# Retention, sparse MoE and slot MoE on one core: x and phi-w2 writes issued later, loads four tiles ahead, end of the branch and slot sums reordered

## The chip, the cores and the metric

The program runs on one core of a Trainium2 chip. The metric is the device time of one execution in microseconds (us); before the change it is 551.8 us, the median of three runs (549.96 to 552.42). Names used below: TensorE (PE) multiplies matrices, VectorE (DVE) and ScalarE (ACT) work elementwise, GpSimd (POOL) works elementwise and issues gathers and scatters, SyncE (SP) issues most of the transfers (DMA). Each engine runs its own instructions in order and waits on semaphores of others.

## The reference

Three layers follow each other. The input is q, k, v of 4 batches, 8 heads, 768 positions and 64 features, and weights in float32.

```python
# 1. retention, head by head, over the sequence
for t in range(S):
    state = gamma * state + k[t] (x) v[t]
    y[t]  = scale * q[t] @ state
x = y, as 3072 tokens x 512 features
# 2. MoE, one expert of 8 per token
e_idx = argmax(x @ w_gate);  gate_w = softmax(x @ w_gate)[e_idx]
eom   = sigmoid(x @ w_output_gate)[e_idx]
out   = gate_w * eom * (relu(x @ w1[e_idx]) @ w2[e_idx])
# 3. slot MoE on that: 8 experts x 4 slots
logits = x @ phi
slots  = softmax(logits, over tokens).T @ x
slots  = relu(slots @ w1[e]) @ w2[e]
out    = softmax(logits, over slots) @ slots
```

## The kernel before

**Stages.** The program has one stage for retention and routing (called the branch here, pool stack `pa`), a conditional part for experts with more tokens than planned (`pv`, not taken with this input), one for the eight experts (`pb`), and one for the slot experts and the output (`pc`). The instructions of an engine stand in the order in which the Python code is written (`manual_schedule`); tile pools set which buffer a tile gets, and an instruction that fills a buffer waits for the last reader of what was in it.

**The branch** goes over 24 tiles of 128 tokens (`NTILE`; 6 chunks of a sequence for each of 4 batches). For a tile i, `load(i)` brings its q, k, v (1 MB, pool `io`); `scores(i)` multiplies k and q, `masks(i)` applies the decay, `out_state` and `out_scores` make the output, and `state` updates the running state. Three tiles are a group (`GROUPS`, `ENDS`): `x_evac` and `x_turn` copy and turn the output, `gate_mm`, `gate_copy`, `gate_sum` make the router's logits, `gate_pick` the choice of expert, `gate_scale` the token's factor, `rank_mm` and `rank` the token's place within its expert. `x_write` multiplies the rows by the factor and stores them to the DRAM tensor `xs` on SP's queue. The list `ORDER` says in which order these steps are written within step i; a name there carries an offset (`"s"` is `scores(i + 1)`, `"xw"` is `x_write(i - 2)`).

Beside this, the branch multiplies phi with the second weights w2 of the eight sparse experts (phi-w2), so that the slot logits can be made from the hidden layer directly. `wq_load(u)` loads a quarter (512 KB) of an expert's transposed w2, 32 quarters in all, `wq_mm(u)` multiplies it, and `wq_put(u)` turns a finished expert and stores it to `wps`. Quarter u is loaded behind step u - 1 and multiplied in step u + 3 (`WLAG`); the quarters that are left behind the last tile follow after the routing.

**End of the branch.** From the ranks a list of rows for each expert is made with the product `lp`, the experts are ordered by their token count (`c8`, `sq8`, `ordf`, `ordi`), and `gather(0)` fetches the rows of the first expert from `xs`, by indirect DMA on POOL. `er` holds the number of the k-th expert in a register of SP, which chooses the weights to load. `limi` holds what the conditional part reads.

**The experts.** Step g = 8 e + f handles block f (128 hidden features) of expert e: `load_w` loads w1 three steps ahead, `split_w` splits it into two parts (ACT and DVE), `l1` makes twelve products and a relu. `behind(e - 1, f)` does the rest of the expert before, a part in each of the eight steps: slot logits, their softmax, `slot_h` (partial sums over tokens, tiles `gps`), `slot_s` (copies `gr` and the sums `gsum`), `slot_t`, and `slot_in` in two halves, which multiplies by w2 (tiles `w`, product `slo`). `load_w2(e, hf)` loads half of w2 (four tiles of 256 KB) into the pool `w2p`, which has four buffers, so a half can be loaded when the half before has been used. `load_m2` brings the weights of the slot experts, up to `NPRE` = 52 of 128 tiles during this stage.

The lines that matter most for SP are the store of x and the loop:

```python
def x_write(i):                       # L547, on SP in step i + 2
    ...
    for a in range(4):
        nc.sync.dma_start(out=xs[...], in_=x[32 * a:32 * a + 32, 0:n]...)   # L557
for i in range(NTILE + 2):            # L579
    load(i + 3)
    for n in ORDER:
        step[n](i)
    ...
    wq_load(i + 1)
```

Of the kernel before, what the change touches and what calls it, by code (L numbers as in the profile page):

```python
# [35 lines left out]
NPRE, NX = 52, 4  # L36
# [99 lines left out]
def retention_moe_kernel(ctx, tc, qt, kt, kn, vn, gates, moe_w1, moe_w2,  # L136
# [47 lines left out]
    whl = ctx.enter_context(tc.tile_pool(name="whl", bufs=3))  # L184
    xp = ctx.enter_context(tc.tile_pool(name="xp", bufs=4))
    xtp = ctx.enter_context(tc.tile_pool(name="xtp", bufs=NX))
# [4 lines left out]
    er = []  # L191
    G = E * KF
# [25 lines left out]


# [27 lines left out]
    with ExitStack() as pa:  # L247
        io = pa.enter_context(tc.tile_pool(name="io", bufs=4))
# [50 lines left out]
        wst = pa.enter_context(tc.tile_pool(name="wst", bufs=6))  # L299
        wtt, wacc = {}, {}  # L300

        def wq_load(u):
            if u < NQ:
                e, q = divmod(u, 4)
                wtt[u] = wst.tile([128, FF], F32, tag="wt", name="wt")
                nc.sync.dma_start(out=wtt[u], in_=moe_w2[1, e, :, q * FF:(q + 1) * FF])

        def wq_mm(u):

            if not 0 <= u < NQ:  # L310
                return
            e, kk = divmod(u, 4)
            if kk == 0:
                wacc[e] = pT.tile([128, 256], F32, tag="w", name="wps")
            t = wtt.pop(u)
            for g in range(4):
                nc.tensor.matmul(out=wacc[e][32 * g:32 * g + 32, :], lhsT=phi[:, kk, :], rhs=t[:, g * 256:g * 256 + 256],  # L317
                                 start=(kk == 0), stop=(kk == KD - 1), skip_group_check=True)

        def wq_put(u):  # L320
            if u % 4 == 3 and 0 <= u < NQ:
                ws = sc2.tile([128, KF, NS], F32, tag="ws", name="ws")
                nc.vector.transpose(out=ws, in_=wacc.pop(u // 4).rearrange("p (f t) -> p f t", t=32))
                nc.sync.dma_start(out=wps[u // 4], in_=ws.rearrange("p f s -> p (f s)"))
# [152 lines left out]
        def gate_pick(i):  # L477
# [5 lines left out]
            lg, og = g[:, :, 0:E], g[:, :, E:2 * E]  # L483
# [3 lines left out]
            nc.vector.tensor_tensor(out=big(1), in0=lg, in1=bc(one_(0), n), op=ALU.subtract)  # L487
            nc.vector.scalar_tensor_tensor(out=big(2), in0=big(1), scalar=0.0, in1=each(con("desc"), n), op0=ALU.is_ge, op1=ALU.mult)
            nc.vector.tensor_reduce(out=one_(3), in_=big(2), axis=AX.X, op=ALU.max)
            nc.vector.tensor_tensor(out=oh[:, t:t + n, :], in0=big(2), in1=bc(one_(3), n), op=ALU.is_equal)  # L490
            for u in range(n):
                nc.vector.tensor_tensor(out=run[:, t + u + 1, :], in0=run[:, t + u, :], in1=oh[:, t + u, :], op=ALU.add)
            nc.vector.tensor_tensor(out=big(4), in0=og, in1=oh[:, t:t + n, :], op=ALU.mult)
            nc.vector.tensor_reduce(out=one_(5), in_=big(4), axis=AX.X, op=ALU.add)
            nc.scalar.activation(out=big(6), in_=big(1), func=ACTF.Exp)
# [15 lines left out]
        def rank_mm(i):  # L511
# [4 lines left out]
            for u in range(n):  # L516
# [3 lines left out]
            nc.tensor.matmul(out=g[:, SC:SC + 4 * n], lhsT=con("same"), rhs=scl.pop(t)[:, 0:n, :],  # L520
                             start=True, stop=True, skip_group_check=True)

        def rank(i):
# [3 lines left out]
            late = t + n == NTILE  # L527
            g = gps.pop(t)
            sm = sc2.tile([128, 3, 4, E], F32, tag="sm2", name="sm2")
            scl[t] = sc2.tile([128, 3, 4], F32, tag="sc", name="sc")  # L530
            nc.vector.tensor_copy(out=scl[t][:, 0:n, :], in_=g[:, SC:SC + 4 * n].rearrange("p (u b) -> p u b", b=4))
# [9 lines left out]
            eng = nc.vector if late else nc.gpsimd  # L541
# [5 lines left out]
        def x_write(i):  # L547
            if i not in ENDS:
                return
            t, n = ENDS[i]  # L550
            s = scl.pop(t)
            x = xr3.pop(t)
            for u in range(n):
                (nc.vector if t + n == NTILE else nc.gpsimd).tensor_tensor(
# [215 lines left out]
    with ExitStack() as pb:  # L770
# [173 lines left out]
        def behind(e, f):  # L944

            if not 0 <= e < E:
                return
# [266 lines left out]
```

## Time and profile before

| What | Value |
|---|---|
| Median of three runs | 551.8 us (549.96 to 552.42) |
| Profiled execution | 553.71 us, its span 551.9 us |
| PE busy | 440.2 us, 80% of the span |
| DVE, ACT, POOL busy | 264.2, 148.3, 129.7 us |
| Moved by DMA | 132.59 MB, mean 240 GB/s |
| SP's queue | 120.24 MB, 63.5% of 16 engines |

The span is the time between the first and the last instruction of the profiled execution; 1.8 us of its time lie outside it. The busy share of an engine is a mean over stages with different limits, so each stage has to be read by itself. "PEclk" in the rows below is the clock that TensorE was granted, as a share of 2.4 GHz (0.50 is 1.2 GHz). "DMA" is the share of time in which the core's 16 DMA engines were busy.

### The profile page before, as it was taken

To read this page: it belongs to the slowest core of one execution; us is meant where nothing else is said; L and a number is where in the kernel's file an instruction comes from. 1 tells how busy PE (TensorE), PEld (TensorE's weight loads), DVE (VectorE), ACT (ScalarE), POOL (GpSimd) and SP (SyncE) were. 2 spreads that over 40 slices of the span, in tenths; PEclk is the share of its full clock that TensorE was granted. 3 is DMA by queue.
4 is the path that set the end of the run, shared out by engine and by line. 5 is a ranking of instruction groups with operands and counts; after the bars stand their busy time and mean duration, and the time that the engine had idled before them with its cause. 6 is when DMAs were issued, how large, how long until landed. Compare 5 with 4: busy or idle time off the path is not lost.

```text
span 551.9 us, 11581 instructions
## 1 busy us (share of the span) xinstructions
PE 440.2 (80%) x4403; PEld 304.2 (55%) x4403; DVE 264.2 (48%) x711; ACT 148.3 (27%) x341; POOL 129.7 (23%) x143
## 2 busy tenths in 40 slices
PE   4793965956856335999999999999999996697993
PEld 3672743645644103888676675867667673234253
DVE  1573744645547501356555546654655654323033
ACT  1431111102102001444344333433334431112033
POOL 2222403504503310203240605124050303020020
PEclk9897878879778555799999999999999999689897
DMA  8957696696674781568293965929395726999958
GB/s 265 399 232 249 214 338 187 240 348 179 261 221 125 209 277 46 160 220 278 90 359 116 313 221 176 331 83 367 106 333 194 268 70 194 364 375 383 361 179 280
DMA packets 71826, 132.59 MB, mean 240 GB/s; under 512 B 8434, under 2 KB 28912, under 8 KB 69456
## 3 DMA queue, kind: packets, MB, share of 16 engines
q1 hardware_dynamic: 65136, 120.24, 63.5%
q0 software_dynamic: 3408, 8.39, 4.4%
q10 hardware_dynamic: 3216, 3.11, 1.7%
q8 instruction: 37, 0.61, 0.5%
q14 instruction: 29, 0.24, 0.1%
HBM read 117.68 MB, written 14.05 MB: 239 GB/s over the span
## 4 chain that ended last, share of the span: by engine, by line
PE 48%; DMA 8%; ACT 2%; DVE 2%; issue 1%; ACTq 0%; SPq 0%
PE hps L809 25%; DMA w<-in_moe_w_dram 5%; PE slo L939 4%; PE gps L918 4%; PE so L1105 3%; PE lps L840 2%; PE fh L1066 2%; PE xps L781 2%; PE ops L1163 1%; DMA ct<-ctok 1%; PE gsum L928 1%; DMA m<-in_moe_w_dram 1%; PE lsum L856 1%; ACT gr L925 1%; PE warm L799 1%; ACT h L814 1%
## 5 line engine op out<-in xcount | busy, mean ns | idle before, releaser
L809 PE MATMUL hps<-xh,wh 128*128 128x416 f32 (+2 forms) x256 | 96.0, 375 | 0.0
L809 PE MATMUL hps<-xh,wl 128*128 128x416 f32 (+2 forms) x256 | 89.6, 350 | 0.0
L809 PE MATMUL hps<-xl,wh 128*128 128x416 f32 (+2 forms) x256 | 89.6, 350 | 0.0
L369 PE MATMUL s<-raw 64*128 64x128 f32 x384 | 36.1, 339 | 41.3 <-DMA raw<-in_qt_dram 11.0
L901 POOL DMA_INDIRECT ctok<-cn,xidx x29 | 28.8, 992 | 170.3 <-DVE cn L898 163.9
L379 DVE TENSOR_TENSOR sS<-s,csa 128x512 f32<-128x512 f32 x48 | 30.9, 686 | 75.1 <-PE s L369 75.1
L216 DVE TENSOR_TENSOR wl<-r,wh 128x512 fp32r<-128x512 f32 x64 | 43.5, 680 | 40.1 <-ACT wh L215 39.7
L809 PEld LDWEIGHTS hps<-xh,wh 128*128 128x128 f32 x256 | 48.7, 190 | 20.9 <-issue 19.6
L814 ACT ACTIVATE h<-hps 128x416 f32<-128x416 f32 (+2 forms) x64 | 32.7, 511 | 99.6 <-PE hps L809 94.7
L369 PEld LDWEIGHTS s<-raw 64*128 64x128 f32 x384 | 30.5, 235 | 43.7 <-issue 36.2
L215 ACT ACTIVATE wh<-r 128x512 fp32r<-128x512 f32 x64 | 39.9, 625 | 52.2 <-ACTq L750 35.3
L809 PEld LDWEIGHTS hps<-xl,wh 128*128 128x128 f32 x256 | 48.9, 191 | 1.7 <-issue 0.8
L809 PEld LDWEIGHTS hps<-xh,wl 128*128 128x128 f32 x256 | 48.6, 190 | 0.8
L632 POOL DMA_INDIRECT xg<-xs,xidx x29 | 30.0, 1035 | 63.6 <-PE xps L781 47.0
L434 ACT COPY xT<-o 128x512 f32<-128x512 f32 x24 | 13.9, 580 | 94.3 <-PE o L402 94.3
L317 PE MATMUL wps<-wt,phi 128*32 128x256 f32 x256 | 26.8, 503 | 15.5 <-DMA wt<-in_moe_w_dram 11.3
L939 PE MATMUL slo<-w,gt 128*32 128x512 f32 x128 | 32.5, 640 | 4.3 <-DMA w<-in_moe_w_dram 3.5
L821 DVE STREAM_TRANSPOSE hB<-h 128x416 f32<-128x416 f32 (+2 forms) x64 | 34.4, 577 | 0.0
L351 POOL TENSOR_TENSOR k<-raw,cs 128x512 f32<-128x512 f32 x20 | 21.0, 1063 | 48.7 <-DMA raw<-in_qt_dram 20.3
L402 PE MATMUL o<-sS,raw 128*64 128x128 f32 x384 | 29.5, 302 | 0.0
L791 DVE TENSOR_TENSOR xl<-xps,xh 128x416 fp32r<-128x416 f32 (+2 forms) x32 | 18.2, 582 | 18.8 <-ACT xh L790 18.2
L1105 PE MATMUL so<-m,hT 128*32 128x320 f32 (+1 forms) x256 | 26.8, 408 | 0.0
(159 smaller groups left out, 575.7 us busy)
## 6 DMA issues: line engine op xcount, KB each, us to landing
m<-in_moe_w_dram SPq DMA_DIRECT2D x128, 256.0 KB, 5.3
wt<-in_moe_w_dram SPq DMA_DIRECT2D x32, 512.0 KB, 7.4
r<-in_moe_w_dram SPq DMA_DIRECT2D x64, 256.0 KB, 4.3
w<-in_moe_w_dram SPq DMA_DIRECT2D x64, 256.0 KB, 4.8
xs<-xr SPq DMA_DIRECT2D x28, 192.0 KB, 3.4
raw<-in_kt_dram SPq DMA_DIRECT2D x5, 1024.0 KB, 8.5
raw<-in_kn_dram SPq DMA_DIRECT2D x5, 1024.0 KB, 9.7
raw<-in_vn_dram SPq DMA_DIRECT2D x5, 1024.0 KB, 9.5
```

The lines of the kernel that those rows point to most:

```text
L215: nc.scalar.activation(out=hi, in_=t, func=ACTF.Copy)
L216: nc.vector.tensor_tensor(out=lo, in0=t, in1=hi, op=ALU.subtract)
L369: nc.tensor.matmul(out=ps[h][:, p, :], lhsT=kq(i, p, 0)[r], rhs=kq(i, p, 1)[r], start=True, stop=True, tile_position=(64 * h, 0), skip_gro ...
L379: nc.vector.tensor_tensor(out=sS[i][:, h], in0=sps.pop((i, h)), in1=con("dm", 128)[:, 4 * h:4 * h + 4, :], op=ALU.mult)
L402: nc.tensor.matmul(out=o_at(i, p, h), lhsT=vals(i, 2 * p + h), rhs=s[:, h, p, :], start=(i % NCH == 0 and n < 4), stop=True, skip_group_ch ...
L632: nc.gpsimd.indirect_dma_start(out=xg[e][j][0:r, :], out_offset=None, in_=xs[:, :], in_offset=bass.IndirectOffsetOnAxis(ap=xidx[0:r, e, j: ...
L809: nc.tensor.matmul(out=ps, lhsT=a[:, kk * 128:(kk + 1) * 128], rhs=x[e][kk][:, 0:c], start=(n == 0), stop=(n == 11))
L814: nc.scalar.activation(out=hs[g][:, 0:c], in_=ps, func=ACTF.Relu)
L821: nc.vector.transpose(out=hB[e][:, 0:NB[e], f, :], in_=hs[e * KF + f][:, 0:c].rearrange("p (b t) -> p b t", t=32))
L901: put = nc.gpsimd.indirect_dma_start(out=ctok[:, :], out_offset=bass.IndirectOffsetOnAxis(ap=xidx[0:r, e, j:j + 1], axis=0), in_=cn[0:r, j ...
L939: nc.tensor.matmul(out=slo[e][32 * i:32 * i + 32, :], lhsT=gts[e][:, hf * 4 + i, :], rhs=w2n[e, hf][i], start=(hf == 0), stop=(hf == 1), s ...
L1105: nc.tensor.matmul(out=so[dh][32 * g:32 * g + 32, :], lhsT=hT[:, f % 4, 32 * hg:32 * hg + 32], rhs=m2_t[64 + e * 8 + f][:, DH[dh]], start= ...
```

## The change

- A fifth buffer for tiles (`io`), and loads four tiles ahead (`load(i + 4)` in step i).
- `x_write` only multiplies (always on POOL); the store is a step of its own, `x_put`, issued at the start of step i + 4. The store of a finished expert's phi-w2 (`wq_put`) is issued at the start of the step behind it.
- `wq_load(i)` at the start of step i, used two steps later (`WLAG` = 2). Only 24 quarters are multiplied in the branch; the eight of the last two experts are loaded in its last steps into 16 buffers of 256 KB (`m2a`, later used for `load_m2`) and multiplied behind the conditional part.
- `rank_mm` and the product that spreads the scale (`scale_mm`) are two steps, behind the phi-w2 product. `gate_pick` is cut in two (`gate_own`), the copy of the scale (`scale_copy`) leaves `rank`.
- At the end of the branch the scale and the store of the last rows go ahead of `rank`, the last store is issued on two queues, and three w1 tiles are loaded ahead of the gather. The numbers of the experts are read one at a time (`load_er`).
- In the experts the slot sums `gsum` go one step behind their copies (`slot_t` in f = 6), the first half of `slot_in` to f = 7 and the second half to f = 1 of the next expert; `load_w2` follows. Four warm-up products instead of eight.

```diff
-WLAG = 3
+WLAG = 2
+NQ0 = NTILE
-ORDER = "xe sc rm s m g1 gc xr w g2 G0 q oq os st G1 rk xw k".split()
-NW0 = 8
+ORDER = "xe sc s m g1 gc xr w rr rs g2 G0 Gb q oq os st G1 rc rk xw k".split()
+ORDER_1 = "xe g1 rr rs rc rk xw gc xr w g2 G0".split()
+NW0 = 4
...
-        io = pa.enter_context(tc.tile_pool(name="io", bufs=4))
+        io = pa.enter_context(tc.tile_pool(name="io", bufs=5))
...
+        def wq_early(u):
+            if NQ0 <= u < NQ:
+                e, q = divmod(u, 4)
+                wtt[u] = []
+                for h in range(2):
+                    t = m2a.tile([128, 512], F32, tag="m2", name="wte")
+                    nc.sync.dma_start(out=t, in_=moe_w2[1, e, :, q * FF + h * 512:q * FF + h * 512 + 512])
+                    wtt[u] += [t[:, 0:256], t[:, 256:512]]
...
+        def x_put(i, queues=(nc.sync,)):
+            if i not in ENDS:
+                return
+            t, n = ENDS[i]
             x = xr3.pop(t)
             for a in range(4):
-                nc.sync.dma_start(
+                queues[a % len(queues)].dma_start(
...
-        for i in range(NTILE + 2):
-            load(i + 3)
-            for n in ORDER:
+        for i in range(NTILE + 1):
+            wq_put()
+            x_put(i - 4)
+            wq_load(i)
+            load(i + 4)
+            if i > NTILE - 4:
+                wq_early(NQ0 + 2 * (i + 3 - NTILE))
+                wq_early(NQ0 + 2 * (i + 3 - NTILE) + 1)
+            for n in ORDER if i < NTILE else ORDER_1:
                 step[n](i)
             decay_table(i + 2)
             if i == 0:
                 late_tables()
-                wq_load(0)
-            wq_load(i + 1)
...
+        scale_copy(i)
+        x_write(i)
+        x_put(i, (nc.sync, nc.scalar))
+        rank(i)
...
+        load_er(0)
+        for g in range(3):
+            load_w(g)
         gather(0)
...
-        for u in range(NTILE + 3, NQ):
-            wq_load(u)
-        for u in range(nq, NQ):
-            wq_mm(u)
-            wq_put(u)
+        wq_turn(NQ0 - 1)
+        wq_put()
...
         def behind(e, f):
+            if f == 1 and 0 < e <= E:
+                slot_in(e - 1, 1)
...
             elif f == 1:
                 logit_sum(e)
-                load_w2(e, 0)
             elif f == 2:
                 p_exp(e)
+                load_w2(e, 0)
...
             elif f == 5:
                 slot_s(e)
-                slot_t(e)
                 c_exp(e)
             elif f == 6:
+                slot_t(e)
+                c_put(e)
+            elif f == 7:
                 slot_in(e, 0)
-                c_put(e)
                 load_w2(e, 1)
-            elif f == 7:
-                slot_in(e, 1)
 
         split_w(0)
+        for u in range(NQ0, NQ):
+            wq_mm(u, ps_1, "lr"[u // 4 % 2])
+            if u % 4 == 3:
+                ws = sp.tile([128, KF, NS], F32, tag="wp", name="ws", bufs=2)
+                nc.vector.transpose(out=ws, in_=wacc.pop(u // 4).rearrange("p (f t) -> p f t", t=32))
+                nc.sync.dma_start(out=wps[u // 4], in_=ws.rearrange("p f s -> p (f s)"))
+        load_er(1)
         keep_warm(w1_t[0][0], NW0, ps_h, "h")
...
         e = E - 1
         logits(e, 1)
         mask(e)
+        slot_in(e - 1, 1)
         load_w2(e, 0)
```

**SP in the middle of the branch.** `xs<-xr` is the store of tiles 6 to 8, `raw` are loads of tiles (the first is tile 13), `wt` a quarter of w2. Before:

```order
L337 DMA raw_831<-in_kn_dram 128x2048
L324 DMA wps_74<-ws_862 128x256
L557 DMA xs_71<-xr_619 32x12x128 x4
L306 DMA wt_913<-in_moe_w2_dram 128x1024
L337 DMA raw_915<-in_kn_dram 128x2048
L306 DMA wt_957<-in_moe_w2_dram 128x1024
L337 DMA raw_959<-in_kn_dram 128x2048
```

Now, from the load of tile 14 on:

```order
L355 DMA raw_837<-in_kn_dram 128x2048
L322 DMA wt_913<-in_moe_w2_dram 128x1024
L355 DMA raw_915<-in_kn_dram 128x2048
L598 DMA xs_71<-xr_623 32x12x128 x4
L322 DMA wt_960<-in_moe_w2_dram 128x1024
L355 DMA raw_962<-in_kn_dram 128x2048
```

The store stood ahead of the load of tile 14; now it stands behind that of tile 15.

**PE behind the conditional part.** `wps<-wte` are products of the last two experts' phi-w2 (their last four of 16 rows are shown), `warm` the warm-up, `xps` the transposes of the gathered rows `xg`. Before:

```order
L670 COMPARE_AND_BRANCH
L670 UNCONDITIONAL_BRANCH
L750 UNCONDITIONAL_BRANCH
L799 MATMUL warm_3740<-wh1_3736 128x512 x8
L781 MATMUL xps_3749<-cs0_65,xg_1934 128x128
```

Now:

```order
L234 MATMUL wps_3749<-wte_1822,phi_75 32x256 x2
L234 MATMUL wps_3749<-wte_1824,phi_75 32x256 x2
L234 MATMUL wps_3749<-wte_1826,phi_75 32x256 x2
L234 MATMUL wps_3749<-wte_1828,phi_75 32x256 x2
L855 MATMUL warm_3779<-wh1_3725 128x512 x4
L837 MATMUL xps_3784<-cs0_65,xg_1977 128x128
```

The products of the last two experts' phi-w2 stand between the conditional part and the warm-up, which has four products instead of eight.

**SP in the experts**, around the end of the second half of expert 0's w2 (tiles `w2`); `r1` is a tile of w1, `m2` one of the slot experts' weights, `wp` the stored phi-w2. Before:

```order
L831 DMA w2_4355<-in_moe_w2_dram 128x512
L206 ISA
L206 DMA r1_4366<-in_moe_w1_dram 128x512
L236 DMA m2_4368<-in_moe2_w1_dram 128x512
L825 ISA
L825 DMA wp_4444<-wps_74 128x256
```

Now:

```order
L887 DMA w2_4471<-in_moe_w2_dram 128x512
L881 ISA
L881 DMA wp_4494<-wps_74 128x256
L196 TENSOR_LOAD ordi_79
L196 ISA x2
L211 ISA
L211 DMA r1_4510<-in_moe_w1_dram 128x512
L253 DMA m2_4512<-in_moe2_w1_dram 128x512
```

The second half is issued at the end of the expert's step 7 instead of step 6, and the load of `wp` and the read of an expert's number now stand between it and the next w1 tile.

## Rows read from the trace of the kernel before

**Rows 1.** Busy us of each engine by window, PE clock, DMA share, GB/s.

```profile
118.34:139.74 21.40, 15.08 (x206) 11.55 (x207) 10.88 (x34) 3.13 (x8) 5.87 (x7) 0.82 0.77 266
...
33.32:47.66 14.34, 12.42 (x207) 9.52 (x206) 10.84 (x34) 3.53 (x10) 5.89 (x7) 1.00 0.42 128
...
221.62:465.05 243.43, 231.79 (x1897) 172.29 (x1897) 131.69 (x299) 95.82 (x205) 64.97 (x59) 0.99 0.63 215
...
480.00:524.00 44.00, 39.31 (x298) 14.40 (x298) 11.35 (x49) 6.03 (x15) 2.98 (x3) 0.92 1.03 376
...
0.00:161.18 161.18, 108.98 (x1618) 85.03 (x1619) 81.94 (x242) 30.24 (x80) 46.09 (x60) 0.86 0.77 265
...
132.00:135.00 3.00, 1.30 (x32) 1.16 (x27) 2.53 (x14) 1.13 (x4) 0.00 (x0) 1.00 0.98 218
...
120.00:123.00 3.00, 3.00 (x34) 1.64 (x34) 2.58 (x6) 0.00 (x0) 0.00 (x0) 0.50 1.03 423
```

The columns are the window, its length, busy us (and instructions) of PE, PE's weight loads, DVE, ACT and POOL, then clock, share and rate.

**Rows 2.** Timeline of SP in the branch: start, us, engine, line, transfer.

```profile
136.06 0.68 SPq L337 DMA_DIRECT2D raw<-in_vn_dram  x1
150.30 2.64 SPq L557 DMA_DIRECT2D xs<-xr  x4
```

**Rows 3.** Timeline of PE in the branch; in brackets idle time before, and its releaser.

```profile
37.07 1.16 PE L369 MATMUL s<-raw 64*128 64x128 f32 x16
...
156.30 0.39 PE L520 MATMUL g<-sb,cs 128*128 128x12 f32 x2 [1.15 <-DVE sb L509]
161.18 2.08 PE L369 MATMUL s<-raw 64*128 64x128 f32 x16 [4.49 <-DMA raw<-in_vn_dram]
```

**Rows 4.** Timeline of the hand-over, several engines.

```profile
169.29 1.09 PE L402 MATMUL o<-sS,raw 128*64 128x128 f32 x16
...
189.91 1.28 POOL L632 DMA_INDIRECT xg<-xs,xidx  x1 [8.58 <-DMA wt<-in_moe_w_dram]
...
199.48 1.08 PE L317 MATMUL wps<-wt,phi 128*32 128x256 f32 x8 [7.38 <-DMA wt<-in_moe_w_dram]
...
207.38 0.16 DVE L660 CAST limi<-lim 1x9 int32<-1x9 f32 x1
211.75 0.63 ACT L215 ACTIVATE wh<-r 128x512 fp32r<-128x512 f32 x1 [35.33 <-ACTq L750]
...
213.62 3.75 PE L799 MATMUL warm<-wh 128*128 128x512 f32 x8 [7.03 <-PEq L750]
...
217.17 4.52 PE L781 MATMUL xps<-cs,xg 128*128 128x128 f32 x16
...
221.62 0.74 PE L809 MATMUL hps<-xh,wh 128*128 128x448 f32 x1
```

**Rows 5.** Waits of PE in the experts: us in total, times, longest us.

```profile
PE gsum L928 <- ACT gr L925: 7.9, 7, 1.1
```

**Rows 6.** What PE's second w2 products (line 939) waited for: us, times.

```profile
  DMA w<-in_moe_w_dram: 20.1, 25
```

**Rows 7.** Chain of waits at the end of expert 0: start, us, what.

```profile
266.91 0.55 ACT gr L925 x2
...
270.60 1.00 PE slo L939 x8
...
273.33 4.75 DMA w<-in_moe_w_dram
...
278.12 1.04 PE slo L939 x2
279.17 2.46 PE hps L809 x12
281.63 0.84 PE lps L840 x8
```

**Rows 8.** Timeline of SP in the experts.

```profile
273.91 0.33 SPq L206 DMA_DIRECT2D r<-in_moe_w_dram  x1
...
457.64 2.38 SPq L831 DMA_DIRECT2D w<-in_moe_w_dram  x4
```

More of the change, by code (lines that the diff above doesn't have):

```diff
@@ L191, in retention_moe_kernel, with load_er @@
     er = []
+    def load_er(k):
+        if k < E:
+            er.append(nc.values_load(ordi[0:1, k:k + 1], engines=[mybir.EngineType.SP], min_val=0, max_val=E - 1))
     G = E * KF
@@ L217, in split_w, with wq_mm @@
         w1_t[g] = (hi, lo)
+    wtt, wacc, wput = {}, {}, {}
+    def wq_mm(u, pool, tag):
+        if not 0 <= u < NQ:
+            return
+        e, kk = divmod(u, 4)
+        if kk == 0:
+            wacc[e] = pool.tile([128, 256], F32, tag=tag, name="wps")
+        for g, t in enumerate(wtt.pop(u)):
+            nc.tensor.matmul(out=wacc[e][32 * g:32 * g + 32, :], lhsT=phi[:, kk, :], rhs=t,
+                             start=(kk == 0), stop=(kk == KD - 1), skip_group_check=True)
     def m2_src(n):
@@ L308, in wq_mm @@
[L308 to L324, printed above, removed]
+                t = wst.tile([128, FF], F32, tag="wt", name="wt")
@@ new lines, in wq_load @@
+                nc.sync.dma_start(out=t, in_=moe_w2[1, e, :, q * FF:(q + 1) * FF])
+                wtt[u] = [t[:, g * 256:g * 256 + 256] for g in range(4)]
+        def wq_early(u):
[6 more added lines that the diff above has]
+                    wtt[u] += [t[:, 0:256], t[:, 256:512]]
@@ L326, in retention_moe_kernel, with wq_turn, wq_put @@
+        def wq_turn(u):
+            if u % 4 == 3 and 0 <= u < NQ0:
+                wput[u // 4] = sc2.tile([128, KF, NS], F32, tag="ws", name="ws")
+                nc.vector.transpose(out=wput[u // 4], in_=wacc.pop(u // 4).rearrange("p (f t) -> p f t", t=32))
+        def wq_put():
+            for e in list(wput):
+                nc.sync.dma_start(out=wps[e], in_=wput.pop(e).rearrange("p f s -> p (f s)"))
         raw, k2, q2, sps, sS, Ops, xT3, xr3, gps, gts, gs, scl, gr, oz = ({} for _ in range(14))
@@ L540, in rank @@
             nc.vector.tensor_tensor(out=hi, in0=ps, in1=lo, op=ALU.subtract)
-            eng = nc.vector if late else nc.gpsimd
-            nc.vector.tensor_tensor(out=lrow[:, t:t + n, :], in0=each(con("i128"), n), in1=bc(lo, n, 128), op=ALU.is_equal)
             nc.vector.tensor_tensor(out=lcol[:, t:t + n, 1, :], in0=each(con("code"), n), in1=bc(hi, n, 32), op=ALU.is_equal)
@@ L574, in retention_moe_kernel @@
         late_consts(1)
+        load(3)
         k_scale(0)
@@ L773, in retention_moe_kernel @@
         ps_1 = pb.enter_context(tc.tile_pool(name="ps_1", bufs=1, space=PSUM))
-        xh, xl, hs, hB, wp, w2n, lps, lrs, lrs2, sms, msks, lms, ces, gps, gts, slo = ({} for _ in range(16))
+        xh, xl, hs, hB, wp, w2n, lps, lrs, lrs2, sms, msks, lms, ces, gps, gts, grs, slo = ({} for _ in range(17))
         puts = {}
@@ L922, in slot_s, with slot_t @@
         def slot_s(e):
-            gr = sp.tile([128, 4, 256], F32, tag="gr", name="gr")
+            grs[e] = sp.tile([128, 4, 256], F32, tag="gr", name="gr")
             for a in range(4):
-                (nc.scalar.copy if a % 2 else nc.vector.tensor_copy)(out=gr[:, a, :], in_=gps[e][a])
+                (nc.scalar.copy if a % 2 else nc.vector.tensor_copy)(out=grs[e][:, a, :], in_=gps[e][a])
+        def slot_t(e):
+            gr = grs.pop(e)
             gps[e] = ps_1.tile([128, 256], F32, tag="D", name="gsum")
@@ L983, in retention_moe_kernel @@
                     gather(e + 1)
+                if e:
+                    load_wp(e)
+                load_er(e + 2)
+            if e == 0 and f == 2:
                 load_wp(e)
```

93 lines of the change are left out of this document (56 added, 37 removed).

## The prediction

> **What bounds the kernel now.** I read the time of each stage first (busy time by windows), then the timelines of the queue that issues most transfers (SP) and of TensorE (PE), then who waited for whom, and last the chain of waits. The kernel has four stretches: the branch (0 to 161 us, until the last tile's scores), a hand-over (to 221.6, the first expert product), the experts (to 465) and the tail (to 551.9).
>
> In the branch no engine is full: of a group of three tiles, 21.40 us, PE is busy 15.08 us, Vector 10.88, and the DMA engines 0.77 of the time [rows 1]. The reader is to see in the SP timeline that SP issues a tile load at 136.06 and then nothing until 150.30: the next instruction is a store of the scaled x, which waits for its data, and all loads stand behind it [rows 2]. PE runs out of tiles: its group ends at 156.7, it starts again at 161.18 behind 4.49 us for a tile, and the first products after that take 2.08 us where they otherwise take 1.16 [rows 3]. A group that met no such wait went by in 14.34 us [rows 1].
>
> In the hand-over the last tile's output is done at 170.4, the gather of the first expert's rows starts at 189.91, and PE waits for phi-w2 tiles (7.38 us before one quarter). The limits that the branch instruction reads are there at 207.54, Scalar is behind the branch at 211.75, and the first expert product starts at 221.62 [rows 4]. The gather was long done by then; it is the last phi-w2 quarters that hold up the branch.
>
> In the experts PE has work nearly all the time, but waits in two places for each expert: for the copies of the slot partials (7.9 us, seven times) [rows 5], and for the second half of the expert's w2 (20.1 us in all) [rows 6]. Both are on the path: the chain goes gr copy, slo, DMA w, slo [rows 7].
>
> The tail is bound by DMA: from 480 to 524 the DMA engines are busy all the time [rows 1].
>
> **The branch.** The stores go two steps later, and loads come four tiles ahead instead of three, into a fifth buffer. A store's data is then ready well before SP reaches it, so the 14 us hole goes. What is late next is DMA work or PE's own pace; I work out both. DMA: 0.77 x 161.18 = 124 us of work up to the last tile's scores. Of this, one group of stores (768 KB at 218 GB/s, 3.6 us) and three phi-w2 quarters (512 KB at 423 GB/s, 1.24 us each) now come behind that tile's load: 124 - 3.6 - 3.7 = 117 us [rows 1]. PE: the 14.34 us contain a wait of 1.15 us as the one before 156.30 [rows 3], which the new order fills with other products, so about 13; tile 5 is scored at 33.3 and tile 23 six groups later, 33.3 + 6 x 13 to 14.3 = 111 to 119 us. The two are nearly equal, so waits of one add to the other, and I take 119 instead of 161.2: **-42 us**. Bounds: 111 if only PE counts, and 132 if the share of DMA time gets only halfway from 0.77 to 1 (117 / 0.885).
>
> Phi-w2 quarters are used two steps behind their load instead of four. A step of 4.8 us gives 9.6 us for 1.24 us of DMA work; where the fuller queue makes the quarter late all the same, that is the DMA bound again, not a further one. The gate's steps cut in two, the rank's masks in another order and the expert numbers read one by one are the same instructions, and Vector has 10.5 us of a group free [rows 1]: 0.
>
> **The hand-over.** The queue is now longer at its end. Behind the last tile's load stand four phi-w2 quarters (5.0 us), two groups of stores (7.2), the 16 early half-quarters of the last two experts (4 MB, 9.9) and the last two groups' stores (3.6): 25.7 us [rows 1]. So the last store lands at about 119 + 25.7 + 2 = 147, and there the gather starts. By dependencies alone it would come at 142: the last output 7 us behind the scores (today 9.2, with about 2 of low clock in it), and 16 us more, some 3 less than today's 19.5, since the scale goes ahead of the rank [rows 4]. The gather issues four transfers of about 1.3 us each, and the last lands about 4.75 us later (I take the w tile's time [rows 7]): 157.
>
> Meanwhile the branch waits for phi-w2 no more: its limits follow the ranking, at about 126 + 17 = 143, and 4.2 us later (211.75 - 207.54) the engines are through: 147. Then PE does the last two experts' phi-w2, eight quarters of 1.08 us: 8.6, to 156; four warm-up products instead of eight, 1.9 us, to 158; and the transposes of x, 4.45 us (217.17 to 221.62), to 162.5 [rows 4]. The products that PE gets here lie beside the gather, and come onto the path if the gather is earlier than I think. First expert product at 162.5 instead of 221.62: -59 in all, of which **-17** here. Bounds: 152 (products at the high clock, gather at 142), and with DMA at 0.885, (117 + 25.7) / 0.885 + 2 + 15 = 178.
>
> **The experts.** The slot sums move a step behind their copies: the 1.1 us go seven times, **-7.9**; a step of 2.46 us then covers 0.55 us of copies. The second half of w2 is still loaded right behind the first half's products, since it uses the same four buffers; only the place where PE asks for it moves. Today two transposes of x and one set of products stand between the halves (an estimate: 2.46 and two quarters of the 4.45 us above, at the high clock about 4.8 us), and the last w2 tile comes 6.5 us behind the first half (271.60 to 278.12). In the new kernel it is two sets and one set of logits, 2.46 + 0.84 + 2.46 = 5.76 us: only some 0.95 more [rows 7]. So of the 20.1 us six times 0.95 = **-5.7** go. Between nothing and 20.1 I take this, the rows being of the same place. For the last expert it turns: the first half now stands behind the last set, and the wait for the second half (457.64 [rows 8] until about 465 [rows 1]) starts one set later, **+2.4**. On SP the next w1 load stands behind the four w2 issues, a wp load and the read of an expert number: it came 2.3 us behind the first half's end (273.91 [rows 8] against 271.60), now about 3.2; with some 5 us to land it is split at 9.5 us, and PE needs it at 10.6 (three sets, logits, sum, second half). I leave **+2** in all for misses. Sum: **-9**, bounds -20 (no wait for w2 left) and +3 (w2 as late as ever).
>
> **The tail** starts its loads when the last expert's second half is done, as today, and its DMA work is the same: 0, bounds -3 and +4.
>
> **Sum.** The profiled execution took 553.7 us (span 551.9). 553.7 - 59 - 9 = 485.7. That execution is 1.9 us above the median of 551.8, so about **484**.
>
> **The rivals.**
> *DMA only half freed.* Loads and stores mixed all the time, in a queue that is always full, keep the share at 0.885. For it: 0.77 is all that a group reaches now, and the tail, with nothing else to do, moves 376 GB/s, not 423 [rows 1]. Against it: in windows of 3 us the share is 0.98 with stores and 1.03 with loads [rows 1]. First expert product at 178: 553.7 - 43.6 - 9 - 1.9 = 499, and 508 with a share of 0.84.
> The Trainium skill, "DMA: Bandwidth & Descriptors" (Specifications), gives about 358 GB/s as what HBM gives one core. By it the 34.6 MB of tiles and phi-w2 up to the last tile would take 97 us instead of 82, some 15 us on my time, as this rival; the 423 GB/s of the window at 120 [rows 1] do not agree with it for one core alone, so I give it 0.02 of this case's chance.
> *Everything hides.* PE sets the pace, the first product comes at 152, and the w2 tiles land sooner because the scatter of the step before is out of their way: 553.7 - 70 - 16 - 1.9 = 466.
> *A new wait in the experts.* SP stands at the later second half, the w1 tile misses its split by 1 to 2 us in each expert, and w2 is waited for as today. The experts gain nothing: 553.7 - 59 + 3 - 1.9 = 496.
> *Slower: TensorE at 1.2 GHz through the branch.* The granted clock of the groups averages 0.82 now, and falls while PE waits for a tile [rows 1, 3]. If a short wait in each step held it low, a group would take 14.34 x 2.08 / 1.16 = 25.7 us, and tile 23 would be scored at 5 + 7.7 x 25.7 = 203: 553.7 + 42 - 17 - 9 - 1.9 = 568. It decides once six of the eight groups run so (187 us). Against it: with waits of about 1.3 us the clock was 1.00 all through 33.32 to 47.66 [rows 1].
>
> **How the numbers follow.** My forecast 0.57 (own range 474 to 494), half-freed DMA 0.17, everything hides 0.15, new wait 0.08, low clock 0.03. A measurement of this kernel tells about 0.5% from no change. Only the low clock is slower; near 552 lies nothing but its edge, 0.01 of it. So faster 0.97, same 0.01, slower 0.02. The range, 464 to 508, leaves out part of the hidden case, the far end of the half-freed one and the low clock.
>
> **What would show it.** SP's hole ahead of the stores gone, and a DMA share of a group near 0.95 at 15 to 16.5 us; scores of tile 23 at 112 to 126; the gather at 142 to 152, behind a store; the first expert product near 162; no wait of the slot sums, and about 1 us for w in the second step of each expert. I am wrong if the share stays at 0.77, if PE waits for split w1 tiles, or if the gather comes more than 33 us behind the last scores.

## The result and the profile after

The changed kernel took 483.29 us (median of 4 runs, 481.69 to 486.3) beside 551.15 us before: ratio 0.8775, 95% interval [0.8726, 0.8824]. Forecast was 484, range 464 to 508. Measured again later, it took 488.93 us (6 runs), ratio 0.8862 [0.8815, 0.8909]. So kernels that were not measured together are told apart only from about 1% on, and below that I go by the stages of the traces.

The profiled execution took 486.3 us, span 484.5. These are the changed kernel's stages by windows (columns as in [rows 1]); they end at the same events as the prediction's: last tile's scores, first expert product, second w2 half of the seventh expert (before, at 465.05, the last of its products still ran until 465.58, so that by its end the experts changed by -6.4 and the tail by -0.4).

```profile
0.00:115.82 115.82, 98.16 (x1619) 77.07 (x1619) 80.67 (x238) 29.33 (x77) 47.88 (x60) 0.99 0.99 363
115.82:161.03 45.21, 22.83 (x281) 14.60 (x278) 23.86 (x91) 6.05 (x16) 12.32 (x15) 0.70 0.69 219
161.03:398.63 237.60, 230.18 (x1900) 169.48 (x1900) 131.87 (x301) 95.93 (x206) 64.74 (x59) 0.99 0.66 223
398.63:484.50 85.87, 66.42 (x606) 28.15 (x606) 25.75 (x82) 16.74 (x42) 7.41 (x11) 0.85 0.91 323
```

| stage, us | before | predicted change | after | measured change | after, measured again |
|---|---|---|---|---|---|
| branch | 161.18 | -42 | 115.82 | -45.4 | 117.06 |
| hand-over | 60.44 | -17 | 45.21 | -15.2 | 45.40 |
| experts | 243.43 | -9 | 237.60 | -5.8 | 239.31 |
| tail | 86.85 | 0 | 85.87 | -1.0 | 86.63 |

**Branch.** The DMA share is 0.99 up to the last scores (before 0.77 [rows 1]), the granted clock 0.99 (0.86). SP's timeline answers to [rows 2]: SP still reaches a store ahead of its data and stands still there, 5.1 us from 77.89 to 82.94 and 6.5 us from 105.14 to 111.62, where it stood 14 us before. Both times the store goes out 0.02 us behind POOL's multiply, which ends at 82.92 and 111.60. But two more tile loads now stand ahead of the store, and the DMA engines stay busy meanwhile: share 1.00 and 0.98 in these two stretches, where it was 0.71 in the 13.6 us of [rows 2]. PE's answers to [rows 3]: the last two tiles are scored in 1.16 us each, behind 0.60 us of waiting at most.

```profile
77.51 0.38 SPq L355 DMA_DIRECT2D raw<-in_vn_dram  x1
82.94 2.82 SPq L598 DMA_DIRECT2D xs<-xr  x4
...
103.78 0.76 SPq L355 DMA_DIRECT2D raw<-in_vn_dram  x1
104.58 0.56 SPq L322 DMA_DIRECT2D wt<-in_moe_w_dram  x1
111.62 2.76 SPq L598 DMA_DIRECT2D xs<-xr  x4
```

```profile
110.42 1.16 PE L387 MATMUL s<-raw 64*128 64x128 f32 x16 [0.60 <-DMA raw<-in_vn_dram]
...
115.82 1.16 PE L387 MATMUL s<-raw 64*128 64x128 f32 x16
```

**Hand-over.** The timeline answers to [rows 4]. The gather starts at 144.65, behind a store, as forecast; the branch's number is there at 140.80; PE starts the early quarters at 146.63, stops after four products for 4.30 us that the profile gives no releaser for, and the first expert product follows at 161.03.

```profile
140.80 0.16 DVE L713 CAST limi<-lim 1x9 int32<-1x9 f32 x1
...
144.65 1.28 POOL L691 DMA_INDIRECT xg<-xs,xidx  x1 [9.38 <-DMA xs<-xr]
...
146.63 1.07 PE L234 MATMUL wps<-wte,phi 128*32 128x256 f32 x4 [10.14 <-PEq L804]
...
152.00 5.40 PE L234 MATMUL wps<-wte,phi 128*32 128x256 f32 x60 [4.30 <-issue]
...
154.80 0.63 ACT L220 ACTIVATE wh<-r 128x512 fp32r<-128x512 f32 x1 [22.34 <-PE wps L234]
...
157.33 1.19 PE L855 MATMUL warm<-wh 128*128 128x512 f32 x4
158.37 2.74 PE L837 MATMUL xps<-cs,xg 128*128 128x128 f32 x16
161.03 0.47 PE L865 MATMUL hps<-xh,wh 128*128 128x448 f32 x1
```

**Experts.** PE's wait of the slot sums [rows 5] is gone. The w2 wait [rows 6] stayed nearly as long (us, times; it adds the waits of the products, 4.6, and of their weight loads, 14.9):

```profile
  DMA w<-in_moe_w_dram: 19.5, 19
```

And ACT waits longer for the w1 tiles than before (16.8 us in 12 there; columns as in [rows 5]):

```profile
ACT wh L220 <- DMA r<-in_moe_w_dram: 57.8, 24, 7.6
```

SP's timeline at the end of the first expert shows that both begin with one load. After a w1 tile and a load of the next layer, at 202.82, SP issues nothing for 9.8 us: the next instruction is the load of w2's second half (L887), which needs the buffers that PE frees at 211.54 + 1.06. Three w1 tiles come late behind it.

```profile
200.95 0.33 SPq L211 DMA_DIRECT2D r<-in_moe_w_dram  x1
201.38 1.44 SPq L253 DMA_DIRECT2D m<-in_moe_w_dram  x1
212.61 2.07 SPq L887 DMA_DIRECT2D w<-in_moe_w_dram  x4
214.88 0.33 SPq L881 DMA_DIRECT2D wp<-wps  x1
216.11 0.34 SPq L211 DMA_DIRECT2D r<-in_moe_w_dram  x1
```

```profile
211.54 1.06 PE L996 MATMUL slo<-w,gt 128*32 128x512 f32 x8
...
218.29 1.92 PE L996 MATMUL slo<-w,gt 128*32 128x512 f32 x6
220.36 1.05 PE L996 MATMUL slo<-w,gt 128*32 128x512 f32 x2 [0.15 <-DMA w<-in_moe_w_dram]
...
222.39 0.64 ACT L220 ACTIVATE wh<-r 128x512 fp32r<-128x512 f32 x1 [5.92 <-DMA r<-in_moe_w_dram]
```

### The profile page after: what moved, and what is told of

The parts are those of the page before. It is cut to its first block, busy times and chain, and to the rows that moved or that the text cites. A ratio compares the mean times of both kernels' runs of the same rounds, so it can differ in the third digit from the quotient of the medians.

```text
span 484.5 us, 11581 instructions
## 1 busy us (share of the span) xinstructions
PE 417.6 (86%) x4399; PEld 289.3 (60%) x4399; DVE 262.2 (54%) x710; ACT 148.1 (31%) x341; POOL 132.3 (27%) x144
## 4 chain that ended last, share of the span: by engine, by line
PE 45%; DMA 11%; DVE 6%; issue 3%; SPq 2%; ACT 2%; ACTq 1%
PE hps L865 20%; DMA r<-in_moe_w_dram 4%; PE so L1175 4%; PE gps L974 4%; PE slo L996 4%; PE xps L837 3%; DMA w<-in_moe_w_dram 3%; DMA m<-in_moe_w_dram 2%; PE fh L1136 2%; PE lps L896 2%; SPq L887 1%; PE wps L234 1%; PE ops L1233 1%; PE gsum L987 1%; DMA ct<-ctok 1%
## 5 line engine op out<-in xcount | busy, mean ns | idle before, releaser
L865 PE MATMUL hps<-xh,wh 128*128 128x416 f32 (+2 forms) x256 | 94.5, 369 | 0.3 <-ACT h L870 0.2
L865 PE MATMUL hps<-xh,wl 128*128 128x416 f32 (+2 forms) x256 | 89.1, 348 | 0.5 <-DVE wl L221 0.4
L865 PE MATMUL hps<-xl,wh 128*128 128x416 f32 (+2 forms) x256 | 88.8, 347 | 0.0
L220 ACT ACTIVATE wh<-r 128x512 fp32r<-128x512 f32 x64 | 40.1, 628 | 82.4 <-DMA r<-in_moe_w_dram 57.8
L865 PEld LDWEIGHTS hps<-xh,wh 128*128 128x128 f32 x256 | 48.0, 188 | 18.6 <-issue 11.3
L865 PEld LDWEIGHTS hps<-xh,wl 128*128 128x128 f32 x256 | 48.1, 188 | 2.3 <-DVE wl L221 1.5
L865 PEld LDWEIGHTS hps<-xl,wh 128*128 128x128 f32 x256 | 48.1, 188 | 1.7 <-issue 0.8
L397 DVE TENSOR_TENSOR sS<-s,csa 128x512 f32<-128x512 f32 x48 | 30.9, 685 | 28.8 <-PE s L387 28.7
L387 PE MATMUL s<-raw 64*128 64x128 f32 x384 | 30.2, 299 | 11.9 <-DMA raw<-in_qt_dram 10.3
L996 PE MATMUL slo<-w,gt 128*32 128x512 f32 x128 | 29.8, 666 | 5.2 <-DMA w<-in_moe_w_dram 4.6
L387 PEld LDWEIGHTS s<-raw 64*128 64x128 f32 x384 | 25.3, 199 | 14.5 <-issue 6.5
L420 PE MATMUL o<-sS,raw 128*64 128x128 f32 x384 | 28.0, 291 | 0.0
L589 POOL TENSOR_TENSOR xr<-xr,sc 128x512 f32<-128x512 f32 x24 | 25.7, 1096 | 2.9 <-DVE sm L569 2.9
L420 PEld LDWEIGHTS o<-sS,raw 128*64 128x64 f32 x384 | 21.9, 144 | 3.9 <-issue 3.6
```

Of the source, the lines that this page charges most:

```text
L220: nc.scalar.activation(out=hi, in_=t, func=ACTF.Copy)
L387: nc.tensor.matmul(out=ps[h][:, p, :], lhsT=kq(i, p, 0)[r], rhs=kq(i, p, 1)[r], start=True, stop=True, tile_position=(64 * h, 0), skip_gro ...
L397: nc.vector.tensor_tensor(out=sS[i][:, h], in0=sps.pop((i, h)), in1=con("dm", 128)[:, 4 * h:4 * h + 4, :], op=ALU.mult)
L420: nc.tensor.matmul(out=o_at(i, p, h), lhsT=vals(i, 2 * p + h), rhs=s[:, h, p, :], start=(i % NCH == 0 and n < 4), stop=True, skip_group_ch ...
L865: nc.tensor.matmul(out=ps, lhsT=a[:, kk * 128:(kk + 1) * 128], rhs=x[e][kk][:, 0:c], start=(n == 0), stop=(n == 11))
L996: nc.tensor.matmul(out=slo[e][32 * i:32 * i + 32, :], lhsT=gts[e][:, hf * 4 + i, :], rhs=w2n[e, hf][i], start=(hf == 0), stop=(hf == 1), s ...
```

## The experiments

Each kernel is the changed one with the edit shown. a1 to a4 were measured together, then a12, b1, b2 and b4, then the changed kernel again with c2, d1a and d1b.

### The branch: stores, loads, both

```diff
 # a1: in x_write, behind the multiply; the late x_put calls but the last go
+            if i < NTILE - 1:
+                x_put(i)
 # a2: three tiles ahead, bufs=4
-        load(3)
-            load(i + 4)
+            load(i + 3)
 # a12: both
```

> The changed kernel with its x stores issued on SP right behind the multiply of x_write again (step xw), loads still four tiles ahead. Theory (SP's order): the store waits on SP for POOL's product and holds back the loads behind it; four tiles of lead cover one more tile of it than three did, so part of the stall returns: scores of the last tile at 130 to 150 us (changed kernel 115.82, before 161.18), DMA share of the branch near 0.8, time 497 to 515 us. Rival (depth): the fourth tile of lead is what removed the holes, the place of the stores is nothing: scores of the last tile at 116 to 119 us, time 483 to 487 us.

> The changed kernel with loads three tiles ahead and four raw buffers, as before; stores stay late. Theory (SP's order): with nothing ahead of the loads that waits, three tiles of lead are enough: scores of the last tile at 116 to 121 us, time 483 to 489 us. Rival (depth): the holes of the branch return, scores of the last tile beyond 135 us, time above 500 us.

> Both parts of the branch's change undone together: x stores on SP right behind the multiply, and loads three tiles ahead with four raw buffers. Each alone moved the scores of the last tile to 130.27 and 128.05 us and cost some 15 us. Theory (one slack, used twice): a wait of a store on SP is covered as long as the loads that stand behind it have lead; with late stores or a fourth tile gone alone half of the cover is left, with both gone none: scores of the last tile at 150 to 161 us, time 518 to 530 us. Rival (two separate costs that add): scores at 142 to 143 us, time 511 to 514 us; what is left to 161 us would then lie with the other moved parts (phi-w2 writes, order of the step).

Measured: a1 499.07 us, ratio 0.904 [0.8974, 0.9107], last scores at 130.27. a2 497.71 us, 0.9009 [0.8936, 0.9081], last scores at 128.05. a12 529.7 us, 0.9623 [0.9559, 0.9686], last scores at 161.77. The first two left me with half a theory: for a2 I had expected the order alone to be enough, and it isn't. The third decides: one slack is used twice. Alone the two undone parts cost 14.5 and 12.2 us of the branch, together 46.0, more than their sum: either part alone keeps 31.5 to 33.7 of the 46.0 us. With both undone the branch is that of before. The SP timeline of a12 has the old holes again, 14 and 15 us long:

```profile
113.65 0.50 SPq L355 DMA_DIRECT2D raw<-in_vn_dram  x1
128.00 2.64 SPq L600 DMA_DIRECT2D xs<-xr  x4
...
135.65 0.74 SPq L355 DMA_DIRECT2D raw<-in_vn_dram  x1
151.16 2.65 SPq L600 DMA_DIRECT2D xs<-xr  x4
```

So the other moved parts of the branch (phi-w2 writes, steps cut in two) bring nothing that can be seen here. From the last scores to the first expert product a12 takes 45.4 us, as the changed kernel does: these two stages don't touch each other.

### The hand-over: the last phi-w2 quarters

```diff
 # a4: no early quarters (NQ0 = NQ, wq_early gone)
+        for u in range(NTILE + 1, NQ):
+            wq_load(u)
+        for u in range(NTILE, NQ):
+            wq_mm(u, pT, "w")
+            ...
 # b4: the same products, but ahead of the branch of the program
-        for u in range(NQ0, NQ):
-            wq_mm(u, ps_1, "lr"[u // 4 % 2])
+        for u in range(NQ0, NQ):     (behind lim and limi, ahead of values_load)
+            wq_mm(u, pT, "w")
+            ...
```

> The changed kernel without the early loads of the last two experts' phi w2: the seven quarters are loaded behind the first w1 tiles and multiplied ahead of the branch of the program, as before. Theory: 3.5 MB at about 0.4 MB a us stand ahead of the branch of the program, the first expert product comes 8 to 14 us later than in the changed kernel (161.03), time 491 to 498 us. Rival (the cover): the hand-over is bounded by the last x store, the gather and the branch, which the phi products only fill: the first expert product within 3 us, time 482 to 487 us.

> The changed kernel with the phi products of the last two experts ahead of the branch of the program, while TensorE waits for the gate's numbers (136 to 146 us), instead of behind it, where they ran from 146.63 to 157.40 with a hole of 4.30 us. The two rows of the check on spilled slots are computed ahead of them on VectorE. Theory (TensorE's order bounds the hand-over): transposes of the gathered rows start when these land, near 155 us instead of 158.37, first expert product at 157 to 158.5 us instead of 161.03, time 479 to 481.5 us. Rival (loads): the quarters land too late to be multiplied ahead of the branch, which then waits for them: first product 161 to 164 us, time 483 to 487 us.

a4: 498.86 us, 0.9047 [0.8979, 0.9115], first expert product at 172.73, 11.5 us more behind the last scores than in the changed kernel; the time is just over what I had expected. The early loads carry most of the hand-over's gain. b4: 486.51 us, 0.8834 [0.878, 0.8887], no difference from the changed kernel. The time is the rival's, but its mechanism isn't. The quarters landed and were multiplied in time; then PE waited for ACT's first instruction behind the branch, which comes at 155.03 here as it comes at 154.80 there, and ran the transposes in 4.52 us instead of 2.74. b4's timeline:

```profile
140.70 3.64 PE L234 MATMUL wps<-wte,phi 128*32 128x256 f32 x32 [4.17 <-issue]
...
144.93 1.96 PE L234 MATMUL wps<-wte,phi 128*32 128x256 f32 x32 [0.59 <-DVE ws L711]
...
155.03 0.63 ACT L220 ACTIVATE wh<-r 128x512 fp32r<-128x512 f32 x1 [22.52 <-SPq L810]
...
155.71 2.08 PE L861 MATMUL warm<-wh 128*128 128x512 f32 x4 [8.82 <-ACT wh L220]
...
157.58 4.52 PE L843 MATMUL xps<-cs,xg 128*128 128x128 f32 x16
...
162.03 0.74 PE L871 MATMUL hps<-xh,wh 128*128 128x448 f32 x1
```

and its windows of the idle time and of what follows: the granted clock there is 0.50, the lower level.

```profile
146.90:155.71 8.81, 0.00 (x1) 0.01 (x1) 0.47 (x2) 0.63 (x1) 2.38 (x3) 0.78 0.54 178
155.71:162.03 6.32, 6.32 (x20) 4.05 (x21) 2.36 (x4) 1.63 (x3) 0.38 (x1) 0.50 0.12 43
```

The products behind the branch of the changed kernel are thus no loss: they fill time in which PE can do nothing else.

### The experts: slot sums and w2

```diff
 # a3: slot_s, slot_t, slot_in and load_w2 in the steps of before
 # b2: only the slot sums
             elif f == 5:
                 slot_s(e)
+                slot_t(e)
 # c2: only the buffers (NPRE 52 to 48, four more loads behind the last expert)
-    w2p = ctx.enter_context(tc.tile_pool(name="w2p", bufs=4))
+    w2p = ctx.enter_context(tc.tile_pool(name="w2p", bufs=8))
 # b1: c2, and load_w2(e, 1) in step 4 instead of 7
```

> The changed kernel with the slot sums and the expert w2 loads and products in the places of the kernel before (slot_t right behind slot_s in step 5, halves of w2 loaded in steps 1 and 6, multiplied in 6 and 7). Theory: the wait of the slot sums for ACT's copy (7.9 us, 7 times) returns and the w2 wait stays near 20 us: stage of the experts 243 us instead of 237.6, time 488 to 491 us. Rival (slack): the PE is paced by the w1 tiles in any case and the slot wait only moves to the wait for ACT's split: time 482 to 485 us.

> The changed kernel with slot_t alone back behind slot_s in step 5; the w2 halves keep the places of the changed kernel. The order of the experts undone as a whole gave 489.6 us and a PE wait of 7.9 us for ACT's copy. Theory: the slot sums carry all of that price and the new places of the w2 halves are worth nothing: time 488 to 491 us, PE waits for ACT's copy 7.9 us in 7, the w2 wait near 20 us. Rival (the w2 halves carry it): 483 to 485 us.

> The changed kernel with eight w2 buffers instead of four (four fewer loads of the next layer in the experts, four more behind the last expert), so that the second half of an expert's w2 is loaded in step 4 rather than 7 and has four steps to land. It takes away the w2 wait that the prediction cut by 5.7 us and that stayed at 19.5 us in 19. Theory (the wait is real): the wait falls under 5 us and the stage of the experts shortens by 3 to 7 us (PE was idle there for 7.4 us in all, 237.60 less 230.18): time 477 to 481 us. Rival (cover): the same bytes come in the same stretch, the w1 tiles land later and the PE waits for the split of them instead: stage 236 to 239 us, time 482 to 485 us.

> The changed kernel itself, beside the kernels of this call on the same chip: 481 to 486 us, ratio to the kernel before 0.873 to 0.883.

> The changed kernel with eight w2 buffers instead of four, but each half of w2 loaded in the step where the changed kernel loads it (2 and 7). With eight buffers and earlier loading together the time was 472.05 us, the w2 wait was gone and ACT's wait for the w1 tiles fell from 57.8 to 7.8 us. Theory (SP's queue): in the changed kernel the first half's load stands on SP until the second half of the expert before is multiplied (4.08 us at 220.44), and the w1 loads behind it come late; more buffers alone take that away: ACT's wait for the w1 tiles falls under 15 us, a w2 wait of the second half stays at 8 to 20 us, time 473 to 479 us. Rival (lead alone): what counted was the earlier second half; the buffers alone leave time at 480 to 485 us and the wait for the w1 tiles above 35 us.

The changed kernel measured again took 488.93 us, more than the 481 to 486 that I had expected. a3: 489.58 us, 0.8858 [0.8796, 0.8921], experts 240.54 us. b2: 493.57 us, 0.8955 [0.8895, 0.9015], experts 244.14. Both have the slot wait of 7.9 us in 7 back. The changed kernel's experts took 237.60 and 239.31 us, so undoing the slot sums alone costs 4.8 to 6.5 us, all that the change brings in this stage. Kernels with the same experts as the changed one, measured together with a3 (a1, a2, a4), took 234.9 to 235.3 us there, and those measured together with b2 (a12, b4) 235.1 and 236.2; against these a3 costs some 5.5 us and b2 8 to 9. b2, slower than I had expected, says that the new places of the w2 halves are worth nothing beside early slot sums: the stage is 3.6 us longer than in a3 (244.14 against 240.54), though its w2 products took less (busy and idle 25.3 + 4.6 us against 28.3 + 3.9).

b1: 472.05 us, 0.8546 [0.849, 0.8602]; c2: 473.3 us, 0.8586 [0.855, 0.8622], beside 488.93 us for the changed kernel measured together with c2. Both are the fastest of this study. c2 alone settles that it is the buffers and not the places of the loads: with those unchanged, the buffers took w2 wait (0.2 us, where my theory had left 8 to 20) and w1 wait (3.2 us) away. The edit also moves four loads of the next layer (1 of the stage's 53 MB) behind the last expert; no run has the buffers without that. SP in c2 issues the second half 7.8 us ahead of the first half's products, and the w1 tiles go on behind it:

```profile
202.14 0.33 SPq L211 DMA_DIRECT2D r<-in_moe_w_dram  x1
...
204.79 0.33 SPq L211 DMA_DIRECT2D r<-in_moe_w_dram  x1
...
205.79 1.90 SPq L887 DMA_DIRECT2D w<-in_moe_w_dram  x4
207.94 0.33 SPq L881 DMA_DIRECT2D wp<-wps  x1
209.11 0.33 SPq L211 DMA_DIRECT2D r<-in_moe_w_dram  x1
```

```profile
213.58 1.07 PE L996 MATMUL slo<-w,gt 128*32 128x512 f32 x8
...
220.29 1.07 PE L996 MATMUL slo<-w,gt 128*32 128x512 f32 x8
```

Its experts' window shows a gain of 15.5 us against 237.60, and of 17.2 against the 239.31 measured together with it; 2.5 us of it go again in the tail (86.63 to 89.13):

```profile
163.08:385.17 222.09, 217.36 (x1899) 168.19 (x1898) 131.81 (x301) 94.42 (x206) 62.77 (x58) 1.00 0.72 232
```

For b1 I had taken PE's idle time, 7.4 us, as the most there was to gain, and was wrong: PE's busy time fell too. The lines of the w2 products (busy us, mean ns, idle before them), first of the changed kernel, then of c2, show where that stood. The waits inside a set of products count as busy: products that wait one by one for their tiles overlap less, six in 1.92 us above where eight take 1.07.

```profile
L996 PE MATMUL slo<-w,gt 128*32 128x512 f32 x112 | 26.6, 629 | 4.6 <-DMA w<-in_moe_w_dram 4.6
```

```profile
L996 PE MATMUL slo<-w,gt 128*32 128x512 f32 x112 | 15.5, 604 | 0.4 <-issue 0.4
```

26.6 - 15.5 + 4.6 - 0.4 = 15.3 us, nearly the whole gain of the stage (against the changed kernel measured again, 25.3 + 5.0, it is 14.4 of 17.2 us). So the gain lies in the w2 products themselves. The late w1 tiles cost PE little: its idle time ahead of the products that use them (hps, L865) is 0.8 us in the changed kernel (2.6 measured again) and 0.0 in c2.

### On top of eight buffers: the hand-over again

```diff
 # d1a: b1, and the last two x_put calls on ScalarE's queue
-        x_put(i - 1)
+        x_put(i - 1, (nc.scalar,))
 # d1b: d1a, and the sort of the experts, their counts and limi ahead of rank(i)
```

> The kernel with eight w2 buffers and the earlier second half (472.05 us), with the last two groups' x stores issued by ScalarE instead of SP, where they stood behind the phi quarters' issues (changed kernel: 138.57 us, the gather waited 9.38 us for them). Theory (the branch of the program bounds the hand-over): the gather starts 3 to 5 us earlier and nothing follows from it, as TensorE goes on at 152 us only: 470.5 to 473.5 us. Rival (the gather bounds it): first expert product 3 us earlier, 468 to 470 us.

> The kernel of the stores on ScalarE (d1a) with the order of the experts, their counts and the check on spilled slots ahead of the last rank on VectorE, so that the number the branch of the program waits for comes some 4 us earlier (changed kernel: 140.80 us) and the gather's indices some 2 us later. Theory (the branch bounds the hand-over): TensorE goes on 2 to 4 us earlier, first expert product at 157 to 159 us instead of 161, time 468 to 470.5 us. Rival (the gather's data bound it): no change to d1a, 470.5 to 474 us.

d1a 475.28 us, 0.8625 [0.8582, 0.8667]; d1b 474.78 us, 0.8601 [0.8561, 0.8641]: neither differs from c2, and both lie above what I had expected. In d1a the gather started no earlier (146.66; b1 146.50), against both theories, and from the last scores to the first expert product it took 47.6 us where b1, on which it stands, took 43.5 and c2 44.4. The four stores now stand on ACT ahead of the last tile's gate:

```profile
134.04 3.73 ACTq L598 DMA_DIRECT2D xs<-xr  x4
...
137.82 0.20 ACT L523 ACTIVATE sm<-sm 128x1 f32<-128x1 f32 x1 [5.32 <-DMA xs<-xr]
```

d1b had the branch's number at 141.63 instead of 146.35 and the stretch at 45.6: 2.0 us back for 4.7 us earlier, in the direction of the theory that the branch bounds it, but too little to show in the time.

## Why the prediction was right, point by point

**Branch, -42: measured -45.4.** The effect was right, DMA work and PE's pace became nearly equal, but the reason was right only in part. I wrote that a store's data "is then ready well before SP reaches it"; it isn't, and SP still stands 5 to 6.5 us at a store. What went is the harm: with two more tile loads ahead of the store the DMA engines have work for as long as SP stands (share 0.98 to 1.00), which a1 and a2 bear out, since later stores and more lead each give most of that cover alone. The prediction had not told the two apart. The last six groups took (115.82 - 31.43) / 6 = 14.1 us each, where I had 14.3, so the waits that I added did come, about 1.1 us a group (PE was idle for 7.4 of the 90.8 us from 25 on); the rest of the 3.2 us is a start that was 1.9 us earlier (31.43 for 33.3).

**Hand-over, -17: measured -15.2.** Gather 144.65 for 147, first expert product 161.03 for 162.5. The time counted from the last scores is 1.7 us longer than forecast: PE began the quarters 30.8 us behind them instead of 28 (its first product came 5.8 us behind the branch's number, where I had 4.2), and the 4.30 us without a releaser were not in my sum; the high clock of most quarters (60 products in 5.40 us) and of the transposes (2.74 us for 4.45), with a shorter warm-up, gave the like of these 4.30 back. The absolute 162.5 was met within 1.5 us partly by luck: the branch ended 3.2 us early, and the hand-over took 1.7 us too long. a4 gives the early quarters 11.5 us of the 15.2.

**Experts, -9: measured -5.8.** The slot term was right: -7.9, and no such wait is left. The term that was mis-sized is the w2 one: "only some 0.95 more [rows 7]. So of the 20.1 us six times 0.95 = -5.7 go", with +2.4 for the last expert. The 20.1 us were not time that PE lost: they add 3.5 us of the products' waits and 16.6 of their weight loads'. What the stage spent on w2 is busy and idle time of its products together, before 29.5 + 3.7 = 33.2 us:

```profile
L939 PE MATMUL slo<-w,gt 128*32 128x512 f32 x112 | 29.5, 605 | 3.7 <-DMA w<-in_moe_w_dram 3.5
```

After it was 26.6 + 4.6 = 31.2, so the later place brought 2.0 us of the 3.3 forecast. In the six other traces with these experts the sum was 28.7 to 30.3, a gain of 2.9 to 4.5, so that one trace does not size this term well. The whole stage ranged from 234.9 to 239.3 us in the seven, -4.1 to -8.6 against 243.4, and the forecast of -9 lies just past the far end of that. In the first expert the distance between the halves came out as worked out, 212.53 to 218.28 (5.75 us, predicted 5.76). But the last w2 tile landed 220.36 - 212.61 = 7.75 us behind the first half, not 6.5 as in [rows 7], so the distance gained was eaten. I had seen what bounds the load, and wrote that the half comes "right behind the first half's products, since it uses the same four buffers"; I did not ask what four more buffers would give. The wait of about 1 us for w in each expert, which I had named as a sign, came out longer in most: the second products took 1.9 to 4.3 us where 1.07 is their time without a wait. For misses I left +2; with -7.9 and -2.0 the stage shows about +4. The w1 load behind the second half came 3.5 us behind the first half's end and was split at 9.8, close to the 3.2 and 9.5 that I had; ACT waits 57.8 us for w1 tiles in all, most of it beside PE's work. PE's idle time fell by 11.64 - 7.42 = 4.2 us where 7.9 went, so some 3.7 us of other waits came in their place, 1.1 of them for w2 (3.5 before, 4.6 after).

**Tail, 0: measured -1.0.**

**The rivals.** Half-freed DMA fell with the share of 0.99. "Everything hides" did not come: the first expert product stood at 161.03, not 152. "A new wait in the experts" was right in half of its mechanism, SP standing at the second half and w2 nearly as late as before, and wrong in its price: PE hardly waits for the w1 tiles, and the experts gained 5.8 us where it had nothing. The low clock did not come: 0.99 through the branch.

**Open.** What stops PE behind the branch of the program is not settled; a kernel without that branch wasn't tried. What holds ACT can be read from the traces: its first instruction there starts 1.40 us after the last transfer of the gather has landed in the changed kernel (153.40, then 154.80), and 1.40 to 1.41 us after it in a1, a2, a3, a12, b1, b2 and c2 as well; in b4 it is 1.78 us (153.25, then 155.03). In a4, where the gather landed at 152.80 and the branch's number came at 159.43, ACT started at 165.59, behind the number. So ACT seems to wait for the gather or for the number, whichever is later, and b4, whose PE waited for ACT, looks bound by the gather and not by the branch. That is read from times; no run takes the gather away.

## What to carry to other kernels

A queue that issues in order is a resource of its own: look for the issue that stands still, ask what it waits for, and count everything behind it, not only the transfer itself. Here a store that waits for its product held up the tile loads behind it, and together that cost 46 us; it still waits, but with more loads ahead of it the wait is covered. A load that waits for its buffer cost 15 us, this time nearly all in its own late tiles and not in the w1 tiles behind it, and four more buffers cured it where another place in the schedule brought 2.0 to 4.5 us. Don't take PE's idle time as the bound of a gain: set the same products beside a run without the wait and look at their busy time too.

## What the runs showed of the hardware

**The stop behind the branch.** In each kernel with quarters behind it, PE did four to seven products and then stopped, without a releaser, for 4.30 us (changed kernel; 3.33 measured again), 3.35 (a3), 3.26 (a1), 2.80 (b1), 3.08 (c2), and 2.46 (b2) to 3.25 (d1a) in the others.

**The rate of one core's transfers.** A window of 3 us in the changed kernel's branch moved 429 GB/s, and the 15 us from 25 to 40 moved 412 (the whole branch, stores and start included, 363):

```profile
26.00:29.00 3.00, 2.83 (x40) 1.81 (x36) 1.86 (x4) 1.06 (x3) 0.00 (x0) 1.00 1.03 429
```

The Trainium skill, "Perfetto Trace Analysis" (Roofline), says that one active core can pull more than its share of 358 GB/s and is bounded by its 16 DMA engines at about 435. The trace agrees with its 429 GB/s. The 15 us that the rule of 358 GB/s would have added to the branch did not come: the last scores stood at 115.82 us, where I had forecast 119 without them.

**A DMA issue does not always cost its engine the same.** One issue on SP takes 0.33 us in many rows; the four stores of d1a took 0.34, 0.72, 1.80 and 0.48 us on ACT and held it for 3.73 us in all, with a DMA share of 0.72 meanwhile. What stretches an issue is not shown.
